# Gelu in two batches instead of three, with every engine's order rewritten, in a gated attention and token-MLP kernel

## The chip, the cores and the metric

The kernel runs on one core of one Trainium2 chip. Its five engines each run their own list of instructions in order: PE (TensorE, matmuls), ACT (ScalarE), DVE (VectorE), POOL (GpSimd) and SP (SyncE, which here only issues DMAs). The metric is the device time of the program in microseconds (us).

## The reference

The input is x, 2048 tokens of 448 features. Two branches are mixed by a gate per token. All tensors are bf16.

```
g = sigmoid((x * gate_w).sum(-1, keepdims=True))
a = attention(x) @ wo      # 16 heads of 28, four segments of 512 tokens
b = token_mlp(x)
out = g * a + (1 - g) * b

# attention, segment s, per head; phi(t) = t + 1 if t > 0 else exp(t)
p     = softmax(q @ k.T * 28**-0.5 + causal_mask)
a_dot = p @ v
a_mem = (phi(q) @ M) / (phi(q) @ z + 1e-6)
o     = sigmoid(beta) * a_mem + (1 - sigmoid(beta)) * a_dot
M, z  = M + phi(k).T @ v, z + phi(k).sum()

# token MLP: mixes over the 2048 tokens, once per feature
h = layernorm(x)
u = gelu(einsum('bsd,sf->bdf', h, w1) + b1)         # 1792 wide
y = einsum('bdf,fs->bds', u, w2) + b2               # back to 2048 tokens
b = y.transpose(0, 2, 1)
```

## The kernel before, in words

Every operation is declared once with `op(...)`: its engine (or two engines that it could run on), what it reads and writes, and a name. The dictionary `ORDER` then gives, for each engine, the names in the sequence in which that engine issues them, and `plan` walks these lists. A word such as `u3-4*2@5` means two successive entries, u3-4 and u3-5, where the first takes PSUM bank 5; `#1` marks the second operation of a name. `finalize` turns the remaining dependencies into semaphore waits. Nothing is scheduled by the hardware: an engine that reaches an entry whose inputs or whose PSUM bank are not ready stands still, and everything behind it in its list too.

The work, by names:

- **Projections.** `lo..`/`hi..` (in `pair`) are half-height matmuls of two projections at once, `pr..` their full-height rest. k, q and v tiles come out as `cpk`, `cpq`, `cpv` (ACT or DVE empties the bank); `gt` is the gate's tanh on ACT. Heads that do not fit in the padded layout are regrouped through DRAM by `gk`/`gq` DMAs.
- **Layer norm** (L891 to L911): `bns`, `bna` statistics and `ln` on DVE, some `ln` on ACT.
- **Attention.** For each of eight pairs of units p there are five score groups `sc{p}_{f}` (L951), each filling PSUM banks 0 to 3; one ACT exponential `exp{p}_{f}` of 128x2048 (L960) empties all four banks at once, and POOL masks the diagonal blocks (L963). `pv{u}` (L987) forms the attention values and `mem{u}` the memory term of unit u; DVE transposes and combines them (`ta` L1003, `tm` L1001, `rec`, `oa`, `om`, `ot`). `mst{s}` builds the memory state (L826).
- **First layer.** `u{ft}-{st}` are the 16 steps of each of the 14 tiles of 128 hidden units (L1059), accumulating in one bank. `ev{ft}` (L1064 on ACT, L1066 on DVE) adds the bias and writes bf16 to `uT`. The Gelu, `gl{lo}` (L1068, ACT), runs in place over a whole batch of tiles: tiles 0 to 4, 5 to 9 and 10 to 13.
- **Second layer.** `y{T}-{ft}` are 14 steps for each of 16 tiles of tokens. The first step of a tile needs all of `uT`. The last tile, y15, is split into columns 0 to 319 (`y15-..`) and 320 to 447 (`y15-..#1`). `wo{T}` is the output projection, `ag{T}` (L1044 on ACT, L1048 on DVE) its gated copy, `fin{T}` (L1082, DVE) the mix, `out{T}` the output DMA (L1086).
- **Weights.** w1 and w2 stream through three slots; SP issues a load when the slot's former readers are done.

The first-layer and second-layer steps, the `wo` tiles and the projections are placed between the score groups in PE's list. All full matmuls go through `mm` (L261), so one line, L264, stands for all of them in the profile. `mm` can cut a 128-wide matmul into four quarter-width ones on 32 columns of the array each. In `plan` (L203 to L210), a stretch of PE entries between two score groups or half-height openings is cut that way where it holds a `pv` or `mst`, which are quarter-width by nature; a list `WIDE` names two more stretches, by their first entry, that are cut too.

In the trace an ACT_TABLE_LOAD stands ahead of each Gelu batch, and another ahead of the first exponential behind it.

Of the kernel before, what the change touches and what calls it, by code (L numbers as in the profile page):

```python
# [74 lines left out]
class Sched:  # L75
# [238 lines left out]
wo9@4 y11-3*2 y8-12 sc7_4@0123 y8-13 y11-5 wo11@4 y11-6 pv14@7 y10-8 y12-0@1 y9-0@2 y11-7*2 y13-0@3 y9-1*4 y13-1 y10-9
y9-5 y10-10 mem14@7 y13-2 mem15@0 y11-9 y12-1 wo10@4 y9-6 y13-3 y12-2 y9-7 y10-11 y12-3 y13-4 y9-8 y11-10 pv15@7
y12-4*2 y9-9 y12-6*2 y9-10*2 y12-8 y13-5 y14-0@7 y11-11*2 y14-1 y15-0@0 y9-12 y11-13 y13-6 y9-13 y10-12*2 y14-2*2
y15-1 y13-7 y15-2 y14-4 y12-9 y13-8*2 y15-3 y14-5 y13-10 y12-10 y14-6 y15-4 y14-7 y12-11 y14-8 y13-11*3 y14-9 wo14@5
y14-10 wo12@6 y15-5 y14-11 wo13@5 y12-12 y14-12*2 wo15@6 y15-6*2 y12-13 y15-8*6 y15-0#1@4 y15-1#1 y15-2#1 y15-3#1
# [4 lines left out]
cpk1_3 cpk1_2 cpk1_0 cpq1_2#1 cpq1_3 cpv1 cpq1_1 cpq1_0 gt1 cpv0 gt0 cpv4 gt5 gt4 cpv6 gt7 cpk2_2 gt6 ln7 exp0_0@6
eq1_2 exp0_1@1 cpk2_0 eq1_0 tb exp0_2@5 ln12 exp0_3@7 ek0_2 exp0_4@3 eq1_1 exp1_0@2 eq1_3 mg exp1_1@4 ek0_3 exp1_2@1
exp1_3@6 ek1_0 exp1_4@0 ek1_1 exp2_0@5 gl0 exp2_1@3 ev6 exp2_2@6 ek1_2 exp2_3@4 eq2_0 exp2_4@2 eq2_2 exp3_0@1 ek1_3
exp3_1@5 gl5 gt8 gt9 ek2_0 exp3_2@6 gt11 gt10 exp3_3@3 eq2_1 exp3_4@2 ev11 exp4_0@4 ek2_1 exp4_1@8 exp4_2@7 exp4_3@3
# [5 lines left out]
wo0 padx2 padk1 bns1 padx0 padk2 xTcp0_00 bns3 xTcp0_10 bns0 cpk0_1 padq0 padq2 padq3 bna1 cpk0_1#1 cpk0_2 gw bna0
bns2 bna2 bna3 vpe0 cpk0_3 cpq0_3 cpq0_1 nmr0 cpv2 ln1 ln3 cpv3 ln2 bns5 bns7 cpq1_2 bna5 bns4 bns8 bns10 bns6 bna4
bna8 bns13 bns15 bns11 bna15 bna6 bna7 bns14 vpe4 bns9 bna11 cpv5 b1c nmr4 bna9 cpv7 bna10 vpe8 mk0_0 b2c bns12 cpk2_3
ln4 bna13 ln5 nmr8 ln6 cpq2_3 ln8 phk0_0 bna12 mk0_1 ln9 bna14 ln10 phk0_1 vpe12 cpk2_1 osl ln11 mq1_2 nmr12 ln15 ln13
ln14 maskg0 ev1 ev0 ta0 mk0_2 oc phk0_2 gm mo mq1_1 ev2 rec0 ob0 oa0 mk0_3 gcol0 mq1_3 ta1 phk0_3 ot0 ev3 mk1_0 rec1
# [875 lines left out]
```

## Time and profile before

| | |
|---|---|
| median of 3 runs | 173.31 us (173.21 to 173.56) |
| the profiled execution | 173.06 us |
| its span, first to last instruction | 171.3 us |
| granted TensorE clock | 1.0 in all of the span |
| POOL busy | 65.8 us |
| HBM read and written | 18.76 MB and 2.36 MB, 123 GB/s |
| ACT table loads in all | 7 |

The profile is of one execution; 1.76 us of its time lie outside the span. Matmuls overlap in the array, so PE's busy time counts the union of overlapping instructions; a matmul of 448 columns is listed at 354 ns although the next one starts sooner. `x88` behind a group counts instructions, four for each quarter-width step. A wait is named after the engine and line that ended it.

### The profile page before, as it was taken

The numbers are of one execution on the slowest core, as the hardware profiler recorded it, in microseconds if no ns is written. First come the engines' busy times: TensorE is split into PE (matmuls) and PEld (weight loads), VectorE is DVE, ScalarE is ACT, GpSimd is POOL, SyncE is SP. The second block draws the span as 40 slices with busy tenths as digits, with TensorE's granted clock in tenths as the row PEclk, the third lists the DMA queues.
The fourth block names the chain that finished last, engine by engine and source line by source line (L and its number), as shares of the span: only waits on it lengthen the run. The fifth ranks groups of instructions, "written<-read, shape, count | busy, mean of one in ns | idle before, by whom it ended". The sixth has DMA issues, their size and how long they took to land.

```text
span 171.3 us, 5964 instructions
## 1 busy us (share of the span) xinstructions
PE 166.4 (97%) x2567; PEld 86.0 (50%) x2573; DVE 144.8 (85%) x313; ACT 122.2 (71%) x126; POOL 65.8 (38%) x98
## 2 busy tenths in 40 slices
PE   8799999999999999999999999999999999999994
PEld 3466544454446445454455345544455444566663
DVE  2679999945878998799879999786898996999864
ACT  3443999999899999898897899968855767410001
POOL 8002041455074034431743580079360836540400
PEclk9999999999999999999999999999999999999999
DMA  5999995795654954690306557013865356023313
GB/s 137 285 165 318 160 300 175 187 258 141 176 139 125 183 114 105 163 247 4 98 0 98 161 147 218 5 31 104 246 173 177 108 162 178 27 61 109 113 52 107
DMA packets 50474, 24.66 MB, mean 144 GB/s; under 512 B 14976, under 2 KB 50208, under 8 KB 50448
## 3 DMA queue, kind: packets, MB, share of 16 engines
q1 hardware_dynamic: 50160, 24.05, 55.0%
q8 instruction: 20, 0.33, 0.8%
q10 hardware_dynamic: 288, 0.23, 0.4%
q14 instruction: 6, 0.05, 0.1%
HBM read 18.76 MB, written 2.36 MB: 123 GB/s over the span
## 4 chain that ended last, share of the span: by engine, by line
PE 91%; DVE 4%; DMA 3%; SPq 1%; issue 1%
PE t L264 77%; PE t L951 7%; PE t L987 5%; DMA t<-in_A_x_dram 3%; PE t L826 1%; DVE t L1048 1%; DVE t L798 1%; DVE t L1014 1%; SPq L505 0%; DVE t L1066 0%; DVE t L1003 0%; PE t L647 0%; DVE t L1001 0%; SPq L500 0%; DVE t L1082 0%
## 5 line engine op out<-in xcount | busy, mean ns | idle before, releaser
L264 PE MATMUL t<-t 128*32 128x448 bf16 (+10 forms) x1833 | 142.4, 346 | 0.7 <-issue 0.3
L264 PEld LDWEIGHTS t<-t 128*32 128x32 bf16 (+2 forms) x1839 | 70.3, 96 | 58.2 <-issue 10.3
L960 ACT ACTIVATE t<-t 128x2048 bf16<-128x2048 f32 x40 | 75.0, 1876 | 12.3 <-PE t L951 10.3
L963 POOL TENSOR_SCALAR_AFFINE_SELECT t<-t 128x512 bf16<-128x512 bf16 x64 | 42.7, 687 | 44.1 <-ACT t L960 43.7
L1018 POOL TENSOR_TENSOR t<-t 128x448 bf16<-128x448 f32 x12 | 14.8, 1239 | 26.7 <-DVE t L1016 13.7
L951 PE MATMUL t<-t 28*128 28x512 bf16 (+3 forms) x256 | 15.8, 301 | 0.0
L1044 ACT ACTIVATE t<-t 128x448 bf16<-128x448 f32 x3 | 2.2, 718 | 17.9 <-PE t L264 17.9
L1066 DVE TENSOR_SCALAR t<-t 128x448 bf16<-128x448 f32 x12 | 8.2, 681 | 6.9 <-PE t L264 6.6
L900 POOL TENSOR_TENSOR t<-t 128x4 f32<-128x4 f32 x4 | 4.3, 1069 | 22.9 <-DVE t L898 22.9
L1003 DVE STREAM_TRANSPOSE t<-t 128x512 f32<-128x512 f32 x16 | 11.2, 703 | 1.8 <-PE t L987 1.7
L1048 DVE TENSOR_SCALAR t<-t 128x448 bf16<-128x448 f32 x13 | 9.5, 737 | 3.1 <-PE t L264 3.0
L951 PEld LDWEIGHTS t<-t 28*128 28x128 bf16 x256 | 4.4, 92 | 14.2 <-ACT t L960 10.3
L1082 DVE SCALAR_TENSOR_TENSOR t<-t 128x448 bf16<-128x448 f32 (+2 forms) x17 | 10.6, 645 | 1.1 <-PE t L264 1.0
L987 PE MATMUL t<-t 128*32 128x512 bf16 (+3 forms) x256 | 11.5, 299 | 0.0
L1024 DVE STREAM_TRANSPOSE t<-t 128x512 bf16<-128x512 bf16 x16 | 11.0, 698 | 0.1
L1014 DVE SCALAR_TENSOR_TENSOR t<-t 128x448 f32<-128x448 f32 x12 | 9.9, 826 | 0.1
L1001 DVE STREAM_TRANSPOSE t<-t 128x512 f32<-128x512 f32 x12 | 8.3, 699 | 1.5 <-PE t L264 1.5
L987 PEld LDWEIGHTS t<-t 128*32 128x32 bf16 x256 | 6.9, 97 | 4.9 <-issue 0.4
L891 DVE BATCH_NORM_STATS2 t<-t 128x6 f32<-128x448 bf16 x16 | 9.2, 607 | 0.0
L781 ACT ACTIVATE t<-t 128x512 bf16<-128x512 bf16 x12 | 7.5, 625 | 2.3 <-DVE t L772 2.3
L761 DVE SCALAR_TENSOR_TENSOR t<-t 128x512 bf16<-128x512 bf16 x12 | 8.7, 723 | 0.0
L1016 DVE TENSOR_TENSOR t<-t 128x448 f32<-128x448 f32 x12 | 8.1, 677 | 0.1
(72 smaller groups left out, 127.9 us busy)
## 6 DMA issues: line engine op xcount, KB each, us to landing
t<-in_B_w_dram SPq DMA_DIRECT2D x52, 256.0 KB, 3.9
out_dram<-t SPq DMA_DIRECT2D x15, 112.0 KB, 2.1
t<-in_A_x_dram SPq DMA_DIRECT2D x3, 448.0 KB, 5.8
t<-in_B_w_dram SPq DMA_DIRECT2D x8, 128.0 KB, 2.9
t<-in_A_wo_dram SPq DMA_DIRECT2D x4, 98.0 KB
t<-in_A_wq_dram SPq DMA_DIRECT2D x1, 336.0 KB, 5.3
t<-in_A_wv_dram SPq DMA_DIRECT2D x1, 336.0 KB, 5.6
spare_heads<-t SPq DMA_DIRECT2D x8, 32.0 KB
```

What stands on the lines that cost most here:

```text
L264: last = e.matmul(out[q], w[:, q], x, skip_group_check=True, **kw)
L891: op("DVE", lambda e: e.bn_stats(st6[:, t, :], xh[:, t, :]), reads=[R_x[t]], writes=[R_st6[t]], name=f"bns{t}", cost=512, prio=P_PROJ - 10 ...
L951: last = e.matmul(bank(fb[hl])[:, c0 : c0 + w], kT[r, hg, s * 512 + j * 128 : s * 512 + j * 128 + 128], qT[r, hg, s * 512 + 128 * j : s * ...
L960: op("ACT", lambda e: e.activation(pslot(g), ps[:, fb[0].bank : fb[0].bank + 4, :], ACT.Exp, scale=SCALE), use=fb, reads=[bres(b) for b in ...
L963: op("POOL", lambda e, c0=c0: e.affine_select(pslot(g)[:, :, c0 : c0 + 128], pslot(g)[:, :, c0 : c0 + 128], pattern=[[0, 4], [1, 128]], co ...
L987: last = e.matmul(bank(cb)[32 * hl : 32 * hl + 32, 128 * j : 512], vaug[:, 4 * s + j, 32 * h : 32 * h + 32], pslot(P_fill[u // 2][f])[:, h ...
L1003: dv(lambda e: e.transpose(t2[:, 0, :], bank(cb)[:, 0:512]), [bres(cb)], [R_tt[tb][0]], "ta", 630, use=(cb,))
L1014: dv(lambda e: e.scalar_tensor_tensor(n3[0], n3[0], oc, rb[0], op0=ALU.mult, op1=ALU.mult), [R_tt[tb][0], R_rec[tb], R_omcol], [R_tt[tb][0 ...
L1018: op("POOL", lambda e: e.tensor_tensor(o3, n3[0], n3[1], op=ALU.add), reads=R_tt[tb], writes=[R_ob[tb]], name=f"o{u}", cost=1280, port=Tru ...
L1024: dv(lambda e: e.transpose(oT[:, hg, s * 512 : s * 512 + 512], o), [R_ob[tb]], qres(hg, s), "ot", 635)
L1048: alt=("DVE", lambda e: e.tensor_scalar(ag(T), bank(b)[:, 0:D], gcol[:, T : T + 1], b2g[:, T : T + 1], op0=ALU.mult, op1=ALU.add), dve_cos ...
L1082: op("DVE", lambda e: e.scalar_tensor_tensor(outst[:, p, c0:c1], bank(b)[:, 0 : c1 - c0], omg[:, T : T + 1], ag(T)[:, c0:c1], op0=ALU.mult ...
```

## The change

- `BATCH` becomes tiles 0 to 6 and 7 to 13: two Gelu operations, `gl0` and `gl7`, in place of `gl0`, `gl5` and `gl10`.
- All five lists of `ORDER` are new. PE, POOL and SP keep the same set of entries in another sequence and with other banks; between ACT and DVE some entries that can run on either change sides.
- `WIDE` and its two stretches are dropped.
- `out11` also waits for the resource that the narrow half of the last tile writes, since that half (`fin15#1`) now comes ahead of the wide one (`fin15`).

The diff, with the lists cut to places that the prediction speaks of (the ends of the lists are in full):

```diff
@@ plan @@
-                    x.cols = x.mode == "x" and (run[0].name in WIDE or any(y.mode == "c" for y in run))
+                    x.cols = x.mode == "x" and any(y.mode == "c" for y in run)
...
-WIDE = ("y1-4", "y0-10",)
...
@@ ORDER, PE @@
-lot2@67 hiq0_1 hit2 lok1_2@24 loq1_2@01 lok1_0@35 hiq1_2 hik1_0 hik1_2 loq1_0@76 lot0@50 hiq1_0 hit0 lot4@21 lot6@43
-hit4 lok2_2@76 btr@0 hit6 prk2_2 prx2_3 u1-0@5 sc0_0@0123 u0-0@4 u1-1 u0-1*2 u1-2*3 u0-3 u1-5 u0-4 u1-6 sc0_1@0123
+lot2@32 hiq0_1 hit2 lok1_0@70 loq1_2@45 hik1_0 loq1_0@26 hiq1_2 lok1_2@17 hiq1_0 hik1_2 lot0@05 btr@6 lot6@34 hit0
+lot4@12 hit6 hit4 lok2_2@67 prx2_3 prk2_2 u1-0@5 u0-0@4*2 u1-1 u0-2*2 sc0_0@0123 lok2_0@67 u0-4 prk2_0 u1-2 prk2_1
...
-u7-4 u4-15 u7-5*2 u6-4*2 u7-7 mst0@7 pv3@0 u6-6 pv2@3 u6-7*3 u7-8 u6-10 loq2_0@57 sc2_1@0123 u7-9 u6-11*3 u7-10 u6-14
+sc2_1@0123 u6-12*4 pv3@5 u7-0@4*3 u8-0@6 loq2_0@31 prq2_1 u7-3 u8-1 prq2_0 u8-2*2 u7-4 u8-4 u7-5 u8-5*3 sc2_2@0123
+loq2_2@75 u7-6 prq2_2h u7-7*2 u8-8*3 u7-9 prq2_2 u7-10*2 u8-11 u7-12 u8-12 u7-13 sc2_3@0123 u8-13*3 wo1@7 u7-14 u9-0@6
...
-wo2@0 u10-0@6 u11-0@4 wo3@2 u11-1*2 u10-1 pv5@3 u11-3 u10-2*2 mem5@7 u11-4*3 sc3_2@0123 lot10@57 u10-4 prt11 u10-5
+sc3_1@0123 u9-12 prt8 u9-13*3 u11-3 prt9 mem5@1 pv5@3 wo3@0 u10-0@6 u11-4 u10-1*3 sc3_2@0123 lot10@57 u11-5 prt10
...
-sc5_0@0123 prq3_1 prq3_0 wo7@4 wo5@7 wo4@1 wo6@3 pv8@4 mem8@5 mem9@6 y0-0@7*4 sc5_1@0123 y0-4*2 y2-0@5*3 y0-6 y2-3
+u13-10 prk3_0 u13-11*5 lok3_2@47 sc5_0@0123 prk3_2 loq3_0@65 prq3_1 prq3_0 prx3_3 wo6@1 pv8@0 wo4@3 wo7@4 pv9@6
+y2-0@5*2 wo5@1 mem8@6 mem9@0 y0-0@7*3 y4-0@4*3 sc5_1@0123 y2-2*2 y1-0@6 y2-4 y1-1 y0-3*2 y1-2 y2-5 y1-3 y4-3
...
-y14-10 wo12@6 y15-5 y14-11 wo13@5 y12-12 y14-12*2 wo15@6 y15-6*2 y12-13 y15-8*6 y15-0#1@4 y15-1#1 y15-2#1 y15-3#1
-y15-4#1 y15-5#1 y15-6#1 y15-7#1 y15-8#1 y15-9#1 y15-10#1 y15-11#1 y15-12#1 y15-13#1
+y13-13 y15-6#1 wo12@6 y15-3 y12-13 y15-4*2 y15-7#1 wo14@2 y14-11*3 y15-8#1 wo15@5 y15-6 y15-9#1 y15-10#1 y15-7
+y15-11#1 y15-8 y15-12#1 y15-9 y15-13#1 y15-10*4
...
@@ ORDER, ACT @@
-exp1_3@6 ek1_0 exp1_4@0 ek1_1 exp2_0@5 gl0 exp2_1@3 ev6 exp2_2@6 ek1_2 exp2_3@4 eq2_0 exp2_4@2 eq2_2 exp3_0@1 ek1_3
-exp3_1@5 gl5 gt8 gt9 ek2_0 exp3_2@6 gt11 gt10 exp3_3@3 eq2_1 exp3_4@2 ev11 exp4_0@4 ek2_1 exp4_1@8 exp4_2@7 exp4_3@3
-exp4_4@1 cpk3_3 exp5_0@2 gl10 ag4 eq3_0 exp5_1@5 eq2_3 ek2_3 exp5_2@6 exp5_3@3 ek2_2 exp5_4@0 exp6_0@8 eq3_1 exp6_1@2
+ek1_1 exp2_0@6 exp2_1@7 gl0 exp2_2@5 ek1_2 exp2_3@4 exp2_4@2 eq2_1 exp3_0@1 exp3_1@7 ek1_3 gt8 ev9 eq2_2 gt9 ag3 eq2_0
+exp3_2@2 gt11 exp3_3@8 exp3_4@3 exp4_0@4 ek2_0 gt10 exp4_1@5 ev10 exp4_2@6 ek2_1 exp4_3@1 exp4_4@7 exp5_0@0 gl7 cpq3_3
+ag4 ag7 eq3_0 exp5_1@5 eq2_3 exp5_2@3 exp5_3@4 ek2_2 exp5_4@6 exp6_0@2 ek2_3 exp6_1@1 eq3_1 exp6_2@3 exp6_3@4 cpq3_2
...
@@ ORDER, DVE @@
+padk2 bns1 wo0 padk1 padx1 xTcp0_00 padk0 padx0 padx2 bns0 xTcp0_10 bns2 bna1 padq0 padq2 maskg0 padq3 cpk0_2 cpk0_1
+cpk0_1#1 cpk0_0#1 bns3 bna0 gw cpk0_2#1 bna2 bna3 vpe0 cpq0_1 cpq0_2 cpv3 nmr0 ln3 cpv2 cpk1_0 bns4 bns7 bns5 bns10
+bns6 bns8 ln0 bna8 bna5 b1c bns11 bna7 bna10 bns9 bna11 bna6 bna4 cpv1 bna9 bns15 b2c vpe4 mk0_0 cpv4 nmr4 mk0_1 ln7
...
-fin14 fin13 fin12 fin15 fin15#1
+fin13 fin12 fin14 ag15 fin15#1 fin15
...
@@ wo_tile / mm1 / mm2 @@
-    BATCH = ((0, 5), (5, 10), (10, 14))
+    BATCH = ((0, 7), (7, 14))
...
-           reads=[R_outst[4 if c0 else p]], name=f"out{T}", dma=True, out=True, cost=500, nbytes=256 * (c1 - c0))
+           reads=[R_outst[4 if c0 else p]] + ([R_outst[4]] if T == 11 else []), name=f"out{T}", dma=True, out=True, cost=500, nbytes=256 * (c1 - c0))
```

More of the change, by code (lines that the diff above doesn't have):

```diff
@@ L314 @@
[L314 to L318, printed above, removed]
@@ L319 @@
-y15-4#1 y15-5#1 y15-6#1 y15-7#1 y15-8#1 y15-9#1 y15-10#1 y15-11#1 y15-12#1 y15-13#1
+warm@3 trx0_0@54 warm2 trx0_1@37 lok0_0@01 hik0_0 lok0_2@67 lok0_0h@53 hik0_2 hik0_0h lox0_3@40 loq0_1@61 gtr@5 hix0_3
+lot2@32 hiq0_1 hit2 lok1_0@70 loq1_2@45 hik1_0 loq1_0@26 hiq1_2 lok1_2@17 hiq1_0 hik1_2 lot0@05 btr@6 lot6@34 hit0
+lot4@12 hit6 hit4 lok2_2@67 prx2_3 prk2_2 u1-0@5 u0-0@4*2 u1-1 u0-2*2 sc0_0@0123 lok2_0@67 u0-4 prk2_0 u1-2 prk2_1
+sc0_1@0123 u1-3 u2-0@6*2 u1-4*2 u2-2*2 u1-6 u0-5 u2-4 u1-7 u0-6 sc0_2@0123 u1-8 u5-0@7 u2-5 u0-7*2 u1-9 u0-9 u1-10
@@ new lines @@
+mem11@6 y4-11 y3-5 sc6_1@0123 y5-0@7 y3-6 y5-1*2 y3-7 y5-3 pv11@6 y4-12*2 y3-8 sc6_2@0123 y3-9*3 y6-0@6*2 y3-12 y5-4*2
+y6-2 y5-6*2 sc6_3@0123 y6-3 y7-0@4 y5-8 y3-13 y5-9*2 y7-1 y6-4 y5-11*2 y7-2 lot14@01 loq3_2@32 y5-13 y7-3 prq3_2
+prq3_2h y6-5 y7-4 prt15 y7-5*2 prt14 y6-6 y7-7 mst2@5 y7-8 sc6_4@0123 lot12@75 y6-7*2 prt13 prt12 y7-9 sc7_0@0123 y6-9
+y7-10*2 y8-0@7 wo8@5 y7-12 y6-10 y7-13 y8-1 sc7_1@0123 y6-11 y8-2 y6-12*2 mem12@4 pv13@5 y8-3*3 sc7_2@0123 y8-6*2
+mem13@4 y8-8 pv12@6 y11-0@5 y8-9*2 y11-1 y8-11 sc7_3@0123 wo9@4 y11-2 y10-0@6*3 y11-3 y8-12*2 sc7_4@0123 wo10@4 y10-3
@@ new lines @@
+y11-4 y10-4 y11-5 pv14@7 y9-0@2*2 y12-0@1 y9-2*2 y13-0@3 wo11@0 y10-5*2 y13-1*2 y12-1 y13-3 y9-4 y11-6 y12-2 mem14@0
+y9-5*3 y11-7*2 pv15@0 mem15@4 y9-8 y10-7*2 y9-9 y10-9 y12-3*2 y9-10 y13-4 y9-11 y12-5 y11-9 y10-10*2 y11-10 y13-5*2
+y9-12*2 y14-0@0*6 y15-0#1@7 y15-1#1 y12-6 y13-7 y12-7 y11-11 y10-12 y15-2#1 y12-8 y15-0@4 y14-6 y11-12 y12-9*2 y14-7
+y13-8*2 y15-1 y14-8 y13-10 y11-13 y12-11 y13-11 y15-2 y13-12 y15-3#1 y14-9 y15-4#1 y15-5#1 y12-12 y10-13 y14-10 wo13@2
+y13-13 y15-6#1 wo12@6 y15-3 y12-13 y15-4*2 y15-7#1 wo14@2 y14-11*3 y15-8#1 wo15@5 y15-6 y15-9#1 y15-10#1 y15-7
@@ L320 @@
+y15-11#1 y15-8 y15-12#1 y15-9 y15-13#1 y15-10*4
 """,
     "ACT": """
-ldx1 ldwkb padx1 xTcp0_01 padk0 xTcp0_11 padq1 cpk0_0 cpk0_2#1 ek0_1 cpk0_0#1 cpq0_2 cpq0_0 gt2 gt3 ln0 cpk1_1 ek0_0
-cpk1_3 cpk1_2 cpk1_0 cpq1_2#1 cpq1_3 cpv1 cpq1_1 cpq1_0 gt1 cpv0 gt0 cpv4 gt5 gt4 cpv6 gt7 cpk2_2 gt6 ln7 exp0_0@6
-eq1_2 exp0_1@1 cpk2_0 eq1_0 tb exp0_2@5 ln12 exp0_3@7 ek0_2 exp0_4@3 eq1_1 exp1_0@2 eq1_3 mg exp1_1@4 ek0_3 exp1_2@1
-exp1_3@6 ek1_0 exp1_4@0 ek1_1 exp2_0@5 gl0 exp2_1@3 ev6 exp2_2@6 ek1_2 exp2_3@4 eq2_0 exp2_4@2 eq2_2 exp3_0@1 ek1_3
@@ L330 @@
 """,
     "DVE": """
[L332 to L336, printed above, removed]
@@ L347 @@
+fin4 ot9 mq3_1 rec10 om10 oa10 phq3_1 oa11 fin3 om11 cpq3_2#1 phq3_0 fin5 cpv15 msta2 ot11 ot10 cpv13 cpv12 mstc2
+mq3_2 gcol3 fin7 ag8 fin6 tm12 eps12 ta13 tm13 mq3_3 ta12 phq3_3 ag9 rec12 eps13 rec13 fin8 om12 om13 oa12 oa13 phq3_2
+ag11 tm14 ot13 ta14 tm15 eps14 eps15 ta15 rec14 oa14 ot12 rec15 om15 oa15 omg3 fin9 ot15 om14 fin11 ot14 fin10 b2g3
+fin13 fin12 fin14 ag15 fin15#1 fin15
 """,
     "POOL": """
-hm0 id0 v0 hm1 hm2 z3_1 id1 mhalf szb z3_0 szg v1 rstd0 rstd4 hs0 hs27 rstd8 rstd12 mask0_2_2 mask0_1_1 mask0_0_0
@@ L355 @@
-mask7_1_1 mask7_2_2 mask7_1_3 mask7_0_0 mask7_2_2#1 o12 mask7_4_1 mask7_4_3 o13 mask7_3_0 o14 o15
+id0 id1 hm0 v0 hm1 z3_1 hm2 z3_0 szb mhalf szg rstd0 v1 rstd4 hs0 hs27 rstd8 rstd12 mask0_2_2 mask0_0_0 mask0_1_1
+mask0_1_3 mask0_2_2#1 mask0_4_1 mask0_3_0 mask0_4_3 mask1_2_2 mask1_2_2#1 mask1_1_1 mask1_3_0 mask1_0_0 mask1_1_3
+mask1_4_1 mask2_0_0 mask1_4_3 mask2_2_2 mask2_1_1 mask2_1_3 mask2_2_2#1 mask2_4_1 mask2_4_3 mask2_3_0 mask3_1_1
+mask3_1_3 mask3_2_2 o4 mask3_0_0 mask3_3_0 mask3_2_2#1 mask3_4_1 mask3_4_3 o5 o6 mask4_1_1 mask4_2_2 o7 mask4_1_3
@@ L356 @@
+mask4_2_2#1 mask4_4_1 mask4_3_0 mask4_0_0 mask5_0_0 mask4_4_3 mask5_1_1 o8 mask5_2_2 mask5_1_3 mask5_2_2#1 mask5_3_0
+mask5_4_1 mask5_4_3 o9 mask6_3_0 mask6_2_2 mask6_0_0 mask6_1_1 o11 o10 mask6_2_2#1 mask6_4_1 mask6_1_3 mask6_4_3
+mask7_1_1 mask7_0_0 mask7_2_2 mask7_2_2#1 mask7_3_0 mask7_1_3 o12 mask7_4_1 mask7_4_3 o13 o15 o14
 """,
```

77 lines of the change are left out of this document (32 added, 45 removed).

## The prediction, written before the changed kernel was run

> **What bounds the kernel now.** I read the page first, for the engines' shares and the engines on the chain that ended last.
>
> ```profile
> span 171.3 us, 5964 instructions
> PE 166.4 (97%) x2567; PEld 86.0 (50%) x2573; DVE 144.8 (85%) x313; ACT 122.2 (71%) x126; POOL 65.8 (38%) x98
> PE 91%; DVE 4%; DMA 3%; SPq 1%; issue 1%
> ```
>
> PE is busy for nearly all of the span and carries 91% of the chain; ACT, which runs the Gelu, has 49.1 us free in total. Matmuls are pipelined, so busy is not yet proof. Next come the waits of PE, and the stretch between the first projection and the last matmul (its length, then the busy time of PE, PEld, DVE, ACT and POOL).
>
> ```profile
> PE t L647 <- DMA t<-in_A_x_dram: 1.0, 1, 1.0
> PE t L606 <- PEq L1197: 0.8, 1, 0.8
> PE t L264 <- issue: 0.3, 2, 0.2
> ```
>
> ```profile
> 7.73:168.92 161.19, 160.46 (x2541) 83.20 (x2545) 141.51 (x305) 119.22 (x122) 62.03 (x82) 1.00 0.56 142
> ```
>
> The two long waits lie ahead of 7.73 us. After that PE shows 161.19 - 160.46 = 0.73 us of gaps, with DVE busy for 141.51 us (88%). Whether the busy time is full of work is read from the pace of the chain of waits.
>
> ```profile
> 11.30 13.05 PE t L264 x134
> 28.78 2.29 PE t L264 x11
> 37.49 0.54 PE t L987 x16
> 41.88 0.33 PE t L951 x8
> 42.21 2.19 PE t L264 x11
> 44.39 0.33 PE t L951 x8
> 105.92 2.19 PE t L264 x44
> 115.17 2.19 PE t L264 x11
> 155.05 13.87 PE t L264 x348
> 168.92 0.02 issue
> 168.95 0.35 DVE t L1082
> ```
>
> L951 is a group of scores, L987 a group of attention values, and L264 the filler between them: first-layer and second-layer steps, projections. Eleven full steps take 2.19 us, 0.199 us each, at 42 and at 115 us alike, and forty-four quarter-width matmuls (eleven steps again) take the same at 106 us. From the first scores on, PE goes from one filler to the next at one pace: the end is set by the amount of PE work, not by what ACT does. The last row shows the exit: PE ends at 168.92 and one DVE operation follows.
>
> The Trainium skill ("Perfetto Trace Analysis", section Identifying the Most-Contended Engine) says that matmul busy time is a bad measure of headroom and that the share of weight loading should be used; by the 50% in the page it would leave PE half free and make ACT and DVE candidates. The pace above speaks against that here: the steps do not stretch where ACT is loaded. What this would give if it held is a rival below.
>
> **The Gelu.** ACT around the first batch, and the rows by shape:
>
> ```profile
> 54.20 1.28 ACT L1068 ACT_TABLE_LOAD   x1
> 55.49 2.07 ACT L1068 ACTIVATE t<-t 128x2240 bf16<-128x2240 bf16 x1
> 57.58 1.28 ACT L960 ACT_TABLE_LOAD   x1
> 58.88 1.88 ACT L960 ACTIVATE t<-t 128x2048 bf16<-128x2048 f32 x1
> ```
>
> ```profile
> L1068 ACT ACTIVATE t<-t 128x2240 bf16<-128x2240 bf16 x2 | 4.1, 2072 | 0.0
> L1068 ACT ACTIVATE t<-t 128x1792 bf16<-128x1792 bf16 x1 | 1.7, 1698 | 0.0
> ```
>
> One tile more costs 2072 - 1698 = 374 ns, so a batch of seven takes 2072 + 2 x 374 = 2820 ns. Before: 2 x 2.07 + 1.70 = 5.84 us; after: 5.64 us. Each batch has a table load into it and one back, 1.28 us each; three batches have six, two have four, so 2.57 us go. ACT saves 2.77 us in all. The new orders also hand 19 small operations from DVE to ACT and 17 from ACT to DVE, which leaves ACT near its old load and DVE a little under it. On PE this is worth nothing by itself, since PE does not stand waiting for ACT; the work that covers it is the filler, and if that cover is gone the price is the lateness below.
>
> The Trainium skill ("ScalarE: Activation LUTs", section What ACT_TABLE_LOAD costs) adds a drain of about 1380 ns to each load of about 1283 ns; by that the two loads would be worth 5.3 us of ACT. The trace has the 1.28, and 0.01 us between load and Gelu, so no such drain; the sum uses the trace.
>
> Does a batch of seven hold PE up? First batch: after the order's sc2_1 come 18 first-layer steps, pv3, one opening pair and six projection matmuls up to sc2_2. The 28.78 row holds three steps, such a pair and six such matmuls; so 2.29 + 15 x 0.199 + 0.54 + 0.33 = 6.15 us. ACT does in that time one exponential, load, Gelu, load: 1.88 + 1.28 + 2.82 + 1.28 = 7.26 us, so the next exponential is 1.1 us late. The score group after that, sc2_3, comes about 3.8 us behind sc2_2 (13 steps 2.6, half-width projections and a pair 0.9, scores 0.33). The late exponential is over at 0.5 + 1.1 + 1.88 = 3.5 us (0.5 from a score's start to its exponential's, as at 78.30 and 78.80 in the rows below), so PE arrives 0.3 us later and does not wait. Second batch: from sc5_0 to y2-0, the first second-layer step, which needs all Gelus, PE has the scores, 12 projection matmuls, an opening pair, 12 steps' worth of wo tiles and two groups of values: 0.33 + 1.69 + 1.36 + 2.39 + 1.08 = 6.85 us (1.69 is 2.29 less three steps). ACT needs 0.5 + 1.88 + 1.28 + 2.82 = 6.48. Cover by 0.2 to 0.4 us, priced at 0; if ACT arrives late at this batch, every tenth beyond that is lost.
>
> **PE's own order.** The same 617 entries stand in both PE lists; no matmul is added. What costs extra is a change between full-height, half-height (projection openings) and score matmuls: a score group streams 512 columns, 0.23 us at the pace of a step (448 in 0.199), and takes 0.33 at 41.88, so a change costs some 0.1 us. I count 93 such changes in the old list and 95 in the new: +0.1 us (0 to +0.2). The dropped WIDE list turned two stretches into quarter-width matmuls; the equal 2.19s price that at 0.
>
> **A wait of before that goes.** One real hold-up on PE is found:
>
> ```profile
> 77.46 0.70 DVE L1003 STREAM_TRANSPOSE t<-t 128x512 f32<-128x512 f32 x1
> 78.09 0.67 DVE L1001 STREAM_TRANSPOSE t<-t 128x512 f32<-128x512 f32 x1
> 78.30 0.40 PE L951 MATMUL t<-t 28*128 28x256 bf16 x8
> 78.80 1.86 ACT L960 ACTIVATE t<-t 128x2048 bf16<-128x2048 f32 x1
> 78.82 0.36 PE L264 MATMUL t<-t 64*128 64x449 bf16 x2
> ```
>
> The scores from 78.30 take 0.33, so PE could go on at 78.63; it goes at 78.82, when the second transpose has emptied bank 7. The new list gives that opening (lot10) the banks of prt8 and prt9, whose evictions have a whole batch of steps for themselves: -0.2 us (-0.3 to 0).
>
> **The tail.** Before, tile y15 ends with its narrow 128-column half; after, the narrow half is finished first and the last steps, y15-10 to y15-13, are those of 320 columns.
>
> ```profile
> L1082 DVE SCALAR_TENSOR_TENSOR t<-t 128x320 bf16<-128x320 f32 x1 | 0.6, 551 | 0.1
> L1082 DVE SCALAR_TENSOR_TENSOR t<-t 128x128 bf16<-128x128 f32 x1 | 0.3, 349 | 0.2 <-PE t L264 0.2
> out_dram<-t SPq DMA_DIRECT2D x1, 80.0 KB, 1.7
> out_dram<-t SPq DMA_DIRECT2D x1, 32.0 KB, 1.5
> ```
>
> Behind the last matmul now stand 0.55 + 1.7 instead of 0.35 + 1.5: +0.4 us (+0.2 to +0.5), with nothing left to hide it. The dependency added to out11 only makes fin15#1 wait for an output whose tile ended over 20 steps, 4 us, earlier: 0.
>
> **New waits.** All queues are shuffled, so every PSUM bank is emptied at a new moment. Two kinds must be bounded. The plain eviction:
>
> ```profile
> L1066 DVE TENSOR_SCALAR t<-t 128x448 bf16<-128x448 f32 x12 | 8.2, 681 | 6.9 <-PE t L264 6.6
> L891 DVE BATCH_NORM_STATS2 t<-t 128x6 f32<-128x448 bf16 x16 | 9.2, 607 | 0.0
> L893 DVE BATCH_NORM_AGGREGATE t<-t 128x2 f32<-128x6 f32 x16 | 2.3, 164 | 0.0
> L907 DVE TENSOR_SCALAR t<-t 128x448 bf16<-128x448 bf16 x13 | 4.7, 384 | 0.1
> ```
>
> A bank is free 0.68 us of DVE after its last matmul, plus two short hand-overs, say 0.9 in all; the new list's closest reuse (u8-15 to u9-0) leaves five steps, 1.0 us. So an eviction that DVE starts at once just fits, and one queued behind another operation costs up to 0.7 us. The second is the start: lok2_2 takes the bank that btr's two copies empty, and the second copy, b2c, stands on DVE behind nine statistics operations and eight aggregations, an ln, two evictions. At busy time by count that is 9 x 0.575 + 8 x 0.14 + 0.36 + 2 x 0.68 = 8.0 us from the end of hik1_0, less where operations overlap; PE has 76 half-height matmuls there, 76 x 0.097 (13.05/134) = 7.4 us. Wait there: 0 to 0.6. Right behind it ACT must empty four more banks before sc0_0. I take 0.3 us for all new waits together, nearest to the one hold-up of 0.2 that the old order has; bounds 0 and 1.3 (both in full).
>
> **Sum** against the profiled execution: 173.06 + 0.1 - 0.2 + 0.4 + 0.3 = 173.66, of which 171.3 + 0.6 is the span and 1.76 lies around it. The three timed runs have their median 0.25 us higher, at 173.31, so the forecast in those terms is 173.9 us. About 0.2%, 0.35 us, is what a measurement of this kernel can tell from no change.
>
> **Rivals.** *Not slower: DVE's waits all fit.* The mechanism is bank reuse: with DVE handing work to ACT, each eviction starts as its bank is released, and none costs PE anything. Then the new waits are 0 to 0.05 and the sum is 173.31 + 0.1 - 0.2 + 0.4 = 173.6, within the measurement. It decides at u8-15 to u9-0 and at lok2_2: if DVE is free there, this holds. For it: only one hold-up in the old list, which is as tight. Against: DVE is 88% busy, and at the start queued solidly. Chance 0.28.
>
> *Faster: ACT sets the end after all.* If PE's pace hid waits for ACT, the 2.77 us saved would come off: 173.31 - 2.8 + 0.4 for the tail = 170.9. The measure of the Trainium skill named above would have it so. For it: PEld is 50%. Against: equal pace of 0.199 everywhere. Chance 0.08.
>
> *The long Gelu blocks.* If the lateness of 1.1 us that load, Gelu and load leave behind is not caught up by the second batch, y2-0 and every step behind it wait, as the first layer is used up by then: 1.1 less the cover of 0.4 is 0.7 us, 174.6 in all. It decides at 0.4 us of lateness at exp5_0. Against: the group after the first batch already has 0.3 us to spare. Chance 0.14.
>
> The forecast, slightly slower by tail and a few tenths of waits, has 0.50. Its own range is 173.5 to 174.3. With the rivals, 173.2 to 174.9 holds eight in ten: below lies the faster case, above the blocked Gelu with more waits. Slower by over 0.2%: 0.44 of the 0.50 and all of the 0.14, 0.58; within 0.2%: 0.28 and the remaining 0.06, less 0.01 for the low edge, 0.33; faster: 0.08 and that 0.01, 0.09.
>
> **What would show it.** Four table loads of 1.28 in place of six behind the first, two Gelus of 2.82; PE between its first projection and last matmul within 0.5 us of 161.19, at 0.199 per step; PE's end between 168.7 and 169.2, followed by a 128x320 operation of 0.55. A step pace below 0.199 or an earlier start of the first projection would prove me wrong, and so would a PE gap of over 0.5 us ahead of the first second-layer step.

## The result, and the profile after

The changed kernel takes 175.14 us (median of 4 runs, 174.75 to 175.18) beside 173.44 us for the kernel before on the same chip (4 runs, 173.21 to 173.62): ratio 1.0097, 95% interval 1.0078 to 1.0116. It is slower by about 1.7 us. The forecast was 173.9 us, 0.6 above the kernel before; 175.14 lies well above the forecast's own range (173.5 to 174.3) and just outside the wide one (173.2 to 174.9). The profiled execution took 175.18 us.

Line numbers are smaller by 3 after the change (L264 stays). The page's head, busy time and chain by engine:

```profile
span 173.5 us, 5727 instructions
PE 167.0 (96%) x2451; PEld 84.6 (49%) x2456; DVE 140.7 (81%) x311; ACT 121.1 (70%) x125; POOL 66.7 (38%) x98
PE 87%; ACT 7%; DMA 3%; issue 1%; SPq 1%; DVE 0%
```

The span is 2.1 us longer (171.33 and 173.46 before rounding). New is ACT with 7% of the chain: before it had no share. The waits of PE, with total, times and longest:

```profile
PE t L644 <- DMA t<-in_A_x_dram: 1.9, 1, 1.9
...
PE t L264 <- DVE t L847: 0.2, 1, 0.2
```

One wait in the middle is new by name (L847). The first row looks like the largest change (1.9 against 1.0), but it is no effect of the change. It is PE's wait for the second group of x transposes. Their rows in the timeline of the changed kernel, and of the first experiment below, whose lists are the same up to 158 us:

```profile
7.53 0.62 PE L644 MATMUL t<-t 128*128 128x128 bf16 x8 [1.87 <-DMA t<-in_A_x_dram]
```

```profile
6.66 0.62 PE L644 MATMUL t<-t 128*128 128x128 bf16 x8 [0.89 <-DMA t<-in_A_x_dram]
```

The load they wait for lands at a different time in each execution. Over the 13 profiles of this case the start lies between 6.66 and 7.62 us, with the old lists at 6.97 to 7.57 and with the new ones at 6.66 to 7.62. From that point on the same lists repeat to about 0.01 us: the first second-layer accumulations of y12 start 141.97 us after it in the changed kernel and 141.96 in that experiment. So below every trace is read from the start of the second x transposes: how long until the last matmul ends, and how long from there to the span's end.

| kernel | second x transposes | from there to PE's end | PE's end to span's end | ratio to before |
|---|---|---|---|---|
| before | 7.18 | 161.72 | 2.44 | 1 |
| after | 7.53 | 163.17 | 2.77 | 1.0097 (1.0078 to 1.0116) |
| e1_tail | 6.66 | 163.16 | 2.82 | 1.0079 (1.0050 to 1.0109) |
| e2_b2c | 6.86 | 163.17 | 2.77 | 1.0094 (1.0061 to 1.0127) |
| e3_mid | 7.26 | 162.48 | 2.77 | 1.0065 (1.0040 to 1.0091) |
| e4_allfix | 7.36 | 162.48 | 2.82 | 1.0057 (1.0038 to 1.0075) |
| e5_start | 7.62 | 162.91 | 2.76 | 1.0087 (1.0060 to 1.0114) |
| e6_tail2 | 7.50 | 163.20 | 2.54 | 1.0101 (1.0080 to 1.0122) |
| e7_three_new | 7.08 | 164.06 | 2.77 | 1.0153 (1.0123 to 1.0183) |
| e8_two_old | 7.57 | 162.82 | 2.38 | 1.0061 (1.0040 to 1.0082) |
| e9_sum | 7.11 | 162.36 | 2.54 | 1.0032 (1.0015 to 1.0050) |
| e10_before_plus | 7.46 | 161.55 | 2.93 | 1.0004 (0.9988 to 1.0021) |
| e11_no_wide | 6.97 | 161.70 | 2.37 | one run |

The times are those of one profiled execution of each kernel; the ratios are of the timed runs. So the change costs 163.17 - 161.72 = 1.45 us on PE's path and 0.33 at the exit, 1.78 together; 0.97% of 173.44 is 1.68. The rest of the 2.1 us of span is the start, 0.35 us later in this execution.

Where does ACT come into the chain? The chain of waits around the second Gelu batch of the changed kernel (start, length, engine and line; PE's next score group is the last row):

```profile
98.78 1.88 ACT t L957
100.65 0.02 issue
100.67 1.28 ACT L1065
101.95 0.01 issue
101.96 2.82 ACT t L1065
104.78 0.03 issue
104.81 0.59 ACT t L722
105.40 0.03 issue
105.42 1.34 ACT t L1041 x2
106.76 0.02 issue
106.78 1.28 ACT L778
108.06 0.01 issue
108.07 0.27 ACT t L778
108.34 0.27 issue
108.61 1.87 ACT t L957
110.48 0.05 issue
110.52 0.40 PE t L948 x8
```

For nearly 12 us ACT runs with one pause of 0.27 us: exponential, load, Gelu, three evictions (cpq3_3, ag4, ag7), load, eq3_0, and only then exp5_1, which empties the banks that sc5_2 needs. PE lost 0.16 us there: from the start of the last step to that of the scores it took 0.25 us more than the step itself, and 0.10 is the rule at such places.

### The profile page after: what moved, and what is told of

The parts are those of the page before. It is cut to its first block, busy times and chain, and to the rows that moved or that the text cites. A ratio compares the mean times of both kernels' runs of the same rounds, so it can differ in the third digit from the quotient of the medians.

```text
span 173.5 us, 5727 instructions
## 1 busy us (share of the span) xinstructions
PE 167.0 (96%) x2451; PEld 84.6 (49%) x2456; DVE 140.7 (81%) x311; ACT 121.1 (70%) x125; POOL 66.7 (38%) x98
## 4 chain that ended last, share of the span: by engine, by line
PE 87%; ACT 7%; DMA 3%; issue 1%; SPq 1%; DVE 0%
PE t L264 73%; PE t L948 7%; PE t L984 5%; DMA t<-in_A_x_dram 3%; ACT t L957 2%; ACT t L1065 2%; PE t L823 1%; ACT t L1041 1%; ACT L778 1%; ACT L1065 1%; SPq L502 1%; PE t L644 0%; ACT t L722 0%; DVE t L1079 0%; SPq L497 0%
## 5 line engine op out<-in xcount | busy, mean ns | idle before, releaser
L264 PE MATMUL t<-t 128*32 128x448 bf16 (+11 forms) x1717 | 143.1, 345 | 0.9 <-issue 0.3
L264 PEld LDWEIGHTS t<-t 128*32 128x32 bf16 (+2 forms) x1722 | 69.2, 97 | 60.4 <-issue 11.5
L960 POOL TENSOR_SCALAR_AFFINE_SELECT t<-t 128x512 bf16<-128x512 bf16 x64 | 43.5, 698 | 54.5 <-ACT t L957 53.9
L1041 ACT ACTIVATE t<-t 128x448 bf16<-128x448 f32 x7 | 5.0, 721 | 17.1 <-PE t L264 17.1
L1063 DVE TENSOR_SCALAR t<-t 128x448 bf16<-128x448 f32 x12 | 8.1, 676 | 10.8 <-PE t L264 10.6
L783 DVE SCALAR_TENSOR_TENSOR t<-t 128x512 bf16<-128x512 bf16 x12 | 9.8, 814 | 0.0
L1011 DVE SCALAR_TENSOR_TENSOR t<-t 128x448 f32<-128x448 f32 x12 | 9.2, 777 | 0.0
L758 DVE SCALAR_TENSOR_TENSOR t<-t 128x512 bf16<-128x512 bf16 x12 | 8.4, 704 | 0.0
L795 DVE CAST t<-t 128x448 bf16<-128x448 f32 x12 | 7.2, 612 | 1.1 <-PE t L264 1.1
L1045 DVE TENSOR_SCALAR t<-t 128x448 bf16<-128x448 f32 x9 | 6.6, 737 | 1.5 <-PE t L264 1.5
```

Source lines behind the costliest of these rows:

```text
L264: last = e.matmul(out[q], w[:, q], x, skip_group_check=True, **kw)
L783: op("DVE", lambda e: e.scalar_tensor_tensor(ph, qs, 0.0, ph, op0=ALU.max, op1=ALU.add), reads=qres(hg, tc) + [R_phq[hg][tc]], writes=[R_p ...
L960: op("POOL", lambda e, c0=c0: e.affine_select(pslot(g)[:, :, c0 : c0 + 128], pslot(g)[:, :, c0 : c0 + 128], pattern=[[0, 4], [1, 128]], co ...
L1011: dv(lambda e: e.scalar_tensor_tensor(n3[0], n3[0], oc, rb[0], op0=ALU.mult, op1=ALU.mult), [R_tt[tb][0], R_rec[tb], R_omcol], [R_tt[tb][0 ...
```

## The experiments

The first four mend, one by one and together, what the comparison of the two traces had shown: time lost at lok2_2, mst2, lot12, sc5_2 and pv15, and the exit.

**e1_tail: the halves of y15 swapped.** In PE's list each `y15-n` becomes `y15-n#1` and the reverse, so that narrow steps come last; the two output DMAs change places with them, and the added wait of out11 goes.

```
-y15-8#1 wo15@5 y15-6 y15-9#1 y15-10#1 y15-7 y15-11#1 y15-8 y15-12#1 y15-9 y15-13#1 y15-10*4
+y15-8 wo15@5 y15-6#1 y15-9 y15-10 y15-7#1 y15-11 y15-8#1 y15-12 y15-9#1 y15-13 y15-10#1 ... y15-13#1
-fin12 fin14 ag15 fin15#1 fin15            (DVE)
+fin12 fin14 ag15 fin15 fin15#1
```

> The changed kernel with the two halves of the last tile exchanged, so that the narrow half of 128 columns comes last again (the list places stay, only the halves swap). Tail theory: the operation and the output behind the last matmul shrink by 0.4 us, 175.14 to about 174.75, with PE's end where it was. Rival, that the output queue hides the difference: 175.1.

The exit stayed at 2.82 us. DVE and PE at the end, first of the changed kernel, then of this run:

```profile
170.24 0.35 DVE L1079 SCALAR_TENSOR_TENSOR t<-t 128x128 bf16<-128x128 f32 x1
170.75 0.55 DVE L1079 SCALAR_TENSOR_TENSOR t<-t 128x320 bf16<-128x320 f32 x1 [0.15 <-PE t L264]
```

```profile
168.74 0.74 DVE L1045 TENSOR_SCALAR t<-t 128x448 bf16<-128x448 f32 x1
169.64 0.81 DVE L1079 SCALAR_TENSOR_TENSOR t<-t 128x320 bf16<-128x320 f32 x2 [0.16 <-PE t L264]
```

The wide half was over only four narrow steps, 0.22 us, ahead of the narrow one, and its output takes 0.55 on DVE. So DVE could start on the two outputs (0.81) only 0.18 us ahead of PE's end, and was over 0.64 us behind it, where the changed kernel needs 0.60. The theory that the form of the last step decides was wrong; that the distance between the halves decides is tested in e6. The ratio of 1.0079 is no gain that can be told from 1.0097: its interval reaches to 1.0109, and the trace shows the same PE time and exit.

**e2_b2c: the late copy moved.** DVE's list:

```
-bna5 b1c bns11 ... cpv1 bna9 bns15 b2c vpe4
+bna5 b1c b2c bns11 ... cpv1 bna9 bns15 vpe4
```

> The changed kernel with one small DVE copy (b2c) moved up behind its neighbour b1c. Hand-over theory: the wait of 0.29 us at lok2_2 goes and nothing later takes its place, 174.85. Rival, that ACT sets the first score group: PE then waits 0.2 to 0.3 us at sc0_0 instead, 175.1.

In the changed kernel b2c (L866) ends at 24.35 and lok2_2's weights load at 24.58:

```profile
24.19 0.16 DVE L866 COPY t<-t 128x16 f32<-128x16 f32 x1
...
24.58 0.12 PEld L264 LDWEIGHTS t<-t 64*128 64x128 bf16 x2 [0.52 <-issue]
```

With b2c early this wait went: counted from lot6, lok2_2 starts 0.29 us earlier. Yet at PE's end nothing was won (163.17). The timeline of this run shows who took it back:

```profile
24.51 0.77 ACT L907 ACTIVATE t<-t 128x448 bf16<-128x448 bf16 x1
...
24.89 0.17 DVE L899 SCALAR_TENSOR_TENSOR t<-t 128x4 f32<-128x4 f32 x1 [0.38 <-POOL t L897]
...
25.16 0.24 ACT L796 ACTIVATE t<-t 128x1 f32<-128x1 f32 x2
...
25.46 0.88 PEld L264 LDWEIGHTS t<-t 128*128 128x128 bf16 x6 [0.50 <-issue]
...
27.04 0.10 PEld L264 LDWEIGHTS t<-t 64*128 64x128 bf16 x2 [0.23 <-DVE t L724]
```

u1-0 (25.46) now waited 0.20 us for the bank that gt1 and gt7 (L796) release, and they stood behind a layer norm (L907) on ACT. lok2_0 (27.04) waited 0.09 more for a cast (L724) on DVE, which had itself stood still for 0.38 us for POOL. The late copy had hidden two later hand-overs that were nearly as late: with the first wait gone, the next two took its place.

**e3_mid: three places of the middle.** mst2 two steps earlier (for the bank that lot12 waits for), eq3_0 behind exp5_2 (mq3_0 follows it on DVE, to just ahead of mq3_1), pv15 one step later.

```
-prt14 y6-6 y7-7 mst2@5 y7-8 sc6_4        +prt14 mst2@5 y6-6 y7-7 y7-8 sc6_4
-y11-7*2 pv15@0 mem15@4 y9-8 y10-7*2      +y11-7*2 y9-8 pv15@0 mem15@4 y10-7*2
-ag4 ag7 eq3_0 exp5_1@5 eq2_3 exp5_2@3    +ag4 ag7 exp5_1@5 eq2_3 exp5_2@3 eq3_0   (ACT)
```

> The changed kernel with three hand-overs in the second half given room: mst2 two steps earlier (0.26 us waited at lot12), eq3_0 behind two exponentials instead of ahead of them (0.16 at sc5_2), pv15 one step later (0.15). Hand-over theory: 0.5 to 0.57 us less, about 174.6. Rival, that the waits only move to the next hand-over: 175.0 to 175.1.

PE's end came 0.69 us earlier, more than the 0.5 to 0.57 expected: the three waits gave 0.16 at sc5_2, 0.26 at lot12 and 0.15 at pv15, together the 0.57, and mst2 itself took 0.12 less. The ratio is 1.0065. The chain around the Gelu is now PE alone; its last rows in this window:

```profile
104.95 2.70 PE t L264 x56
107.65 0.33 PE t L948 x8
107.98 2.19 PE t L264 x11
110.17 0.33 PE t L948 x8
```

and lot12's bank, emptied by msta2 (L847), is free in time. First the changed kernel, then this run:

```profile
133.70 0.29 DVE L847 TENSOR_TENSOR t<-t 128x128 f32<-128x128 f32 x1 [0.63 <-PE t L823]
...
134.05 0.66 PE L264 MATMUL t<-t 64*128 64x449 bf16 x3 [0.19 <-DVE t L847]
```

```profile
132.78 0.29 DVE L847 TENSOR_TENSOR t<-t 128x128 f32<-128x128 f32 x1 [0.51 <-PE t L823]
...
133.24 1.42 PE L264 MATMUL t<-t 64*128 64x449 bf16 x7
```

What mst2 loses is not a wait for another engine. Its 64 short matmuls in the kernel before, in the changed kernel and in this run:

```profile
130.34 0.67 PE L826 MATMUL t<-t 128*32 128x32 bf16 x64
```

```profile
132.45 0.88 PE L823 MATMUL t<-t 128*32 128x32 bf16 x64
```

```profile
131.64 0.76 PE L823 MATMUL t<-t 128*32 128x32 bf16 x64
```

In the changed kernel nearly all of the 0.20 us lies in two gaps, ahead of the 61st and the 62nd of these matmuls, while the program has waits only ahead of the first. In the profiles with the new lists mst2 takes 0.2 us longer than before (0.1 where it stands two steps earlier), and in none with the old ones; the cause stays open.

**e4_allfix: the edits of e1, e2 and e3 together.**

> All edits of the three kernels above together. If the waits add up one by one: 0.4 + 0.29 + 0.55 less, about 173.9, still some 0.4 us over the kernel before. If the Gelu batch or the length of ACT's work sets the time: 174.8 or more.

It gave what e3 alone gives, as e1 and e2 give nothing: 162.48 and 2.82, ratio 1.0057. The expected time was too low by about what these two were to add.

**e5_start: the whole start.** Beside b2c, what stood behind it:

```
-bna4 cpv1 bna9 bns15 b2c vpe4                        (DVE; b2c goes behind b1c)
+bna4 vpe4 cpv1 bna9 bns15
-cpv0 cpv7 cpv6 ln2 gt1 gt7 cpk2_3 gt4 cpk2_2 gt0 gt6 gt5 ln6     (ACT)
+cpv0 cpv7 cpv6 gt1 gt7 gt0 gt6 ln2 cpk2_3 gt4 cpk2_2 gt5 ln6
```

> The changed kernel with three edits of its start: b2c stands right behind b1c and vpe4 right behind bna4 in DVE's list, and gt1 gt7 gt0 gt6 stand ahead of ln2 in ACT's list. Moving b2c alone took 0.29 us from the wait of lok2_2, but 0.20 came back at u1-0 (its bank is emptied by gt1, queued on ACT behind ln2) and 0.09 at lok2_0 (DVE's cast cpq2_3, queued behind a 0.38 us idle time in which DVE waits for POOL's rstd4). Theory, three separate queue places: with all three mended nothing comes back, PE is 0.35 to 0.45 us earlier at u0-4 than in the changed kernel, measured from the second x transposes, and at its end; ratio to the kernel before about 1.0075. Rival, the stretch is bound by the sum of DVE's and ACT's work, whatever its order: the wait turns up at sc0_0 or at u0-4, the gain is under 0.1 us and the ratio stays at 1.009 to 1.010.

Between the two theories: PE's end is 0.25 us earlier, not 0.35 to 0.45. lok2_2, u1-0 and lok2_0 no longer wait, but 0.1 came back at sc0_0, whose banks wait for the last tanh, gt5:

```profile
27.16 0.16 ACT L796 ACTIVATE t<-t 128x1 f32<-128x1 f32 x1
...
27.37 0.10 PEld L948 LDWEIGHTS t<-t 28*128 28x128 bf16 x4 [0.47 <-ACT t L796]
```

**e6_tail2: the wide half early.** As e1 (with its changes at DVE, SP and out11), but wo15 followed by all wide steps left, and these by the last eleven narrow ones.

```
+wo12@6 y12-13 y15-7 wo14@2 y14-11*3 wo15@5 y15-8 y15-9 y15-10 y15-11 y15-12 y15-13 y15-3#1 y15-4#1 ... y15-13#1
```

> The changed kernel with its last tile put so that all wide steps of y15 come ahead of the last eleven narrow ones (11 x 0.056 = 0.6 us), and wo15 a little earlier. Swapping the halves alone left the time from PE's end to the span's end at 2.8 us, because the wide output (0.55 us on DVE) was released only 0.2 us ahead of the narrow one, and behind ag15. Theory, what counts is that the wide output is over when the last narrow step ends: from PE's end to the span's end 2.4 to 2.45 us as in the kernel before, in place of 2.77; 0.35 us off, ratio about 1.0077. Rival, ag15 (0.74 us, released by wo15) or the waits that the new order of wo14 and wo15 adds hold the outputs up: under 0.1 us off, ratio 1.009 to 1.010.

From the last matmul to the last DVE operation it is 0.40 us, as before the change (0.60 after). The exit is 2.54 us, shorter by 0.23 instead of 0.35: the rest lies in the last transfer. The timed ratio, 1.0101, cannot see it.

**e7_three_new: three Gelu batches in the new lists.** The batches are five, five and four tiles; the last two run back to back where the changed kernel has its second.

```
-BATCH = ((0, 7), (7, 14))        +BATCH = ((0, 5), (5, 10), (10, 14))
-gl7 cpq3_3                       +gl5 gl10 cpq3_3        (ACT)
```

> The orders of the changed kernel, but three Gelu batches again: the first of five tiles where its first batch stands, the second (five) and third (four) back to back where its second batch stands, so the table loads stay four. ACT's work in the second place is 2.07 + 1.70 = 3.77 us in place of 2.82. Theory, the second batch has just 0.26 us of cover (y2-0 starts 0.26 us after the Gelu's end in the changed kernel) and sc5_2 already waits 0.16 us for exp5_1: y2-0 then waits about 0.7 us, and the whole comes 0.9 to 1.0 us later than the changed kernel; ratio about 1.0150. Rival, PE has enough filler there and the count and place of batches do not matter: within 0.2 us of the changed kernel, ratio 1.009 to 1.011.

PE's end is 0.89 us later, ratio 1.0153. The place is y2-0, the first second-layer step:

```profile
101.55 3.66 ACT L1065 ACTIVATE t<-t 128x2240 bf16<-128x2240 bf16 x2
...
105.36 2.89 PE L264 MATMUL t<-t 128*32 128x448 bf16 x56 [0.55 <-ACT t L1065]
```

The two batches take 0.84 us more than the one (3.66 for 2.82); 0.73 of it comes out at y2-0 and 0.11 at sc5_2, as against the changed kernel. y2-0 starts 0.15 us behind the Gelu's end here, and it waits for nothing else; so of the 0.26 us in the changed kernel 0.15 is the hand-over and only 0.11 was cover. The first batch is 0.75 us shorter than in the changed kernel, and PE is no earlier behind it.

**e8_two_old: two batches in the old lists.**

```
-BATCH = ((0, 5), (5, 10), (10, 14))   +BATCH = ((0, 7), (7, 14))
-exp2_0@5 gl0 exp2_1                   +exp2_0@5 exp2_1            (ACT)
-exp3_1@5 gl5 gt8                      +exp3_1@5 gl0 gt8
-exp5_0@2 gl10 ag4                     +exp5_0@2 gl7 ag4
```

> The orders of the kernel before, with nothing changed but the Gelu: two batches of seven, the first at the place of the old second batch, the second at the place of the old third. Theory, the batches need orders of their own: the last Gelu ends 0.75 us later than in the kernel before (2.82 in place of 1.70 us, less what the first places give back), y0-0, the first second-layer step, waits some 0.85 us and sc3_3 some 0.1: slower than the kernel before by 0.8 to 1.0 us, ratio about 1.005. Rival, the Gelu alone costs nothing because ACT is 2.8 us less loaded: ratio 0.999 to 1.001. Second rival, ACT sets the end: faster by over 1 us, ratio under 0.995.

PE's end is 162.82 - 161.72 = 1.10 us later, a little more than the 0.8 to 1.0 expected; ratio 1.0061. 0.92 us are lost at y0-0, at 106.14 below, and 0.15 around mem5 and lot10:

```profile
103.22 2.82 ACT L1068 ACTIVATE t<-t 128x3136 bf16<-128x3136 bf16 x1
...
106.14 0.94 PE L264 MATMUL t<-t 128*32 128x448 bf16 x16 [0.75 <-issue]
```

So two batches at these places cost 1.1 us when the lists stay. With its new lists the cover ahead of the first second-layer step is enough, but waits elsewhere cost more. Two batches at other places of the old lists were not run.

**e9_sum: e3, e5 and e6 together.**

> The changed kernel with the three edits of the middle (0.68 us in its own run), the three of the start (0.25 us at PE's end in their own run) and the last tile put so that its wide output is over early (0.20 us in its own run). Theory, the waits are separate and add up: the span from the second x transposes to the end is 165.93 - 0.68 - 0.25 - 0.20 = 164.8 us, against 164.16 in the kernel before; ratio about 1.004. What is left, about 0.6 us, would be two more mode switches, waits of under 0.1 us each, and no longer any wait of 0.15 us or more that the kernel before does not have. Rival, a wait removed early is paid again later, as b2c's was: over 165.2 us, ratio 1.006 or more.

From the second x transposes to the end it is 162.36 + 2.54 = 164.9 us (expected 164.8), ratio 1.0032. The parts add up but for about 0.1 us: of the start's gain 0.07 came back at pv2 and 0.10 at sc6_4, whose banks are emptied by a tanh on ACT. PE has no named wait left behind the start, although such losses remain, as PE counts as busy while its last matmul still runs:

```profile
PE t L603 <- PEq L1194: 0.8, 1, 0.8
PE t L644 <- DMA t<-in_A_x_dram: 0.4, 1, 0.4
```

**e10_before_plus: the kernel before, mended.** PE's list alone:

```
-sc3_2@0123 lot10@57 u10-4 prt11           +sc3_2@0123 u10-4 lot10@57 prt11
-y10-8 y12-0@1 y9-0@2 y11-7*2 y13-0@3      +y10-8 y11-7*2 y12-0@1 y9-0@2 y13-0@3
```

> The kernel before with its own two waits mended in PE's list alone: lot10 one step later (behind u10-4), y12-0 and y9-0 two steps later (behind y11-7 and y11-8). Theory, PE's end comes earlier by what waits there less what the changed neighbours cost: 0.30 us over a plain step at sc3_2 to lot10 less one more switch of 0.1 to 0.2, and 0.08 at y12-0: 0.1 to 0.2 us off, span from the second x transposes 163.95 to 164.05 us, ratio 0.999, which the timed runs cannot tell from 1. Rival, the bank that is late is needed by the next step as well: 0 or slower, 164.15 to 164.3 us.

PE's end came 0.17 us earlier, as expected. To the span's end it was 164.48 us and not 163.95 to 164.05, because in the profiled execution 2.5 us passed from the last DVE operation to the span's end instead of 2.0. The ratio is 1.0004 (0.9988 to 1.0021). No version here beats the kernel before by an amount that can be measured.

**e11_no_wide: the kernel before with an empty WIDE list** (`WIDE = ()`).

> The kernel before with an empty WIDE list, so that two stretches of second-layer steps go as full-width matmuls instead of quarter-width ones, as in the changed kernel. Theory: 0 on the time, since eleven steps take 2.19 us in either form; span from the second x transposes within 0.03 us of 164.16. Rival: the quarter-width form saves or costs part of a switch beside attention groups, 0.1 to 0.2 us.

161.70 against 161.72 us to PE's end: nothing, as expected. (To the span's end it is 0.09 us less, by the exit.)

## Why the prediction was wrong in size

The direction, and the reason that the saving on ACT brings nothing, were right. The step that failed is the last term of the sum: "I take 0.3 us for all new waits together, nearest to the one hold-up of 0.2 that the old order has; bounds 0 and 1.3". Read against the trace of before, the new waits are 0.29 at lok2_2, 0.11 at lok2_0, 0.26 at lot12, 0.16 at sc5_2, 0.15 at pv15, and 0.08, 0.05 and 0.03 at u1-8, mem5 and pv1: 1.13 us, 0.8 above the value taken. The bound of 1.3 priced one late eviction (0.7) and one place at the start (0.6) in full; there were eight places instead, none over 0.3. Another 0.20 us, inside mst2, is in no term. The waits at lot12, sc5_2 and pv15 are shown by taking them away (e3), those of the start in part (e2, e5); the three small ones are only read off.

With e3, e5 and e6 together (e9) PE's path is 163.17 - 162.36 = 0.81 us shorter than after the change and still 0.64 longer than before. Of the 1.45 us, 1.13 are the waits and 0.20 is mst2; 0.27 went by hold-ups of before that are gone. So 0.39 is left: about 0.2 for two more changes between full-height, half-height and score matmuls (below), and about 0.2 that was not found (mst0 and mst1 have 0.03 each of it). Point by point:

- **PE bounds the kernel: right.** Eleven full steps still take 2.19 us, as in the chain of e3 above, and every wait that was removed without a successor came out at PE's end. The prediction's 0.199 us per step is the mean of such a group and holds a change of kind; from start to start the traces have 0.189. The sum is not touched by this. The Trainium skill ("Perfetto Trace Analysis", section Identifying the Most-Contended Engine) names the share of weight loading as a measure of headroom, beside MFU (the arithmetic done as a share of the peak); that share alone, 49% here, would leave room on PE, and this is not borne out. MFU was not worked out.
- **The Gelu: right.** A batch takes 2.82 us and two loads have gone. ACT stands idle for 0.02 us ahead of a load and 0.01 behind it, so the drain that the Trainium skill ("ScalarE: Activation LUTs", section What ACT_TABLE_LOAD costs) adds to each load does not show after the change either.
- **"Cover by 0.2 to 0.4 us, priced at 0": right for y2-0 in that it does not wait, but tighter than said, and incomplete for the batch.** y2-0 starts at 105.04, 0.26 us behind the Gelu's end at 104.78; by e7 only 0.11 of this was cover. And for this batch I followed only that step, and not the exponential behind it, as I had for the first batch. With three evictions and eq3_0 ahead of it, exp5_1 was late by 0.16 us for sc5_2. The rival of the long Gelu blocks thus holds at another place than it named and at a quarter of its price; e7 and e8 show that its mechanism is real.
- **lok2_2, "0 to 0.6": right,** with 0.29. Its remedy was not in the prediction: e2 shows two more late hand-overs behind it, u1-0 and lok2_0.
- **u8-15 to u9-0: right.** u9-0 starts 1.13 us behind u8-15, with five steps between them, and without a wait. The closest bank reuse was not where waits came from. lok2_2, lok2_0, lot12 and pv15 wait for banks whose emptying operations stand late in DVE's list (b2c, cpq2_3, msta2, tm14), and sc5_2 for a late exponential; apart from b2c I had looked for evictions of first-layer tiles. (tm14 for pv15 is read off the lists; the trace names a POOL operation that ended 0.03 us later.)
- **The hold-up at lot10: right,** 0.19 gone; another of 0.08 at y12-0, which I had not found, went too.
- **WIDE at 0: right** (e11). **Mode switches, +0.1: a little low.** The traces of before and after have 93 and 95 changes, as counted. The last step ahead of the scores at 117.28 us before starts 0.285 us ahead of them, against 0.189 between two steps, and nearly all other changes cost 0.10 to 0.11 too. So two more are an estimated 0.2 us, the upper bound given. No run tests it.
- **The tail, +0.4: nearly right.** 0.33 in the profiles, of which 0.20 is DVE's and is shown by e6. The other 0.13 is less than the last transfer varies by itself.
- **The +0.25 for the median** is of the size that the start's wandering makes, and no error of a step.
- **The signs.** Five table loads in all, two Gelus of 2.82 us and the 128x320 operation of 0.55 us at the end came as said. PE's end at 170.70 instead of 168.7 to 169.2 did not, nor did its path within 0.5 us of the old one.

The rival that DVE's waits all fit fell at lok2_2 and lot12, and the rival that ACT sets the end fell with e8: two loads less made nothing faster.

## What to carry to other kernels

When all queues of a saturated kernel are rewritten, price new waits by the number of hand-overs that change, not by the waits that the tuned old order has left: that order shows the few that survived. Here eight small ones, of 0.03 to 0.29 us, made 1.13. For a long block on an engine, follow every consumer of what is queued behind the block, not only the consumer of the block. And after a wait is taken away look at the next two places in the list before booking the gain: the copy moved early in e2 was worth nothing alone.

## What the runs showed of the hardware

Where two kernels have the same lists, PE's path from the second x transposes on repeats to about 0.01 us between their profiled executions (141.97 and 141.96 us to y12); the larger differences lie at the two ends. The start moves by 0.96 us (6.66 to 7.62), with the landing of one load. From the last DVE operation to the span's end it took 1.97 to 2.53 us. So a trace settles 0.1 us in the middle of this kernel, where three to five rounds of timing leave an interval 0.3 to 0.7% wide, 0.6 to 1.1 us.

PE can also stand still inside one operation that has no wait in the program: about 0.2 us among the 64 short matmuls of mst2, in all six traces of the new lists that leave it at its place, and in none of the four of the old lists. What holds it there is not known.
